# Two attention stages in a written order, with value matmuls side by side, and maximum matmuls over 65 partitions

## The chip, the cores and the metric

The kernel runs on one core of one Trainium2 chip. The metric is device time in microseconds (us), the median of timed executions; lower is better. Beside the timed executions there is one profiled execution, and every row below comes from it. The engines are TensorE (PE in the profile; PEld is its weight load), VectorE (DVE), ScalarE (ACT), GpSimd (POOL) and SyncE (SP, which issues most transfers).

## The reference

Three layers follow one another on inputs of 2 batches with 768 tokens each.

```python
# 1: attention, 8 heads of 64, a query sees the keys of its own hash bucket
q_bits = (np.einsum('bhsd,dk->bhsk', q, proj) > 0)
k_bits = (np.einsum('bhsd,dk->bhsk', k, proj) > 0)
mask = q_bucket[:, :, :, None] == k_bucket[:, :, None, :]
scores = np.where(mask, scale * np.matmul(q, k.transpose(0, 1, 3, 2)), -1e9)
attn = np.exp(scores - np.max(scores, axis=-1, keepdims=True))
attn = attn / (np.sum(attn, axis=-1, keepdims=True) + 1e-09)
x = np.matmul(attn, v)
# 2: one of 8 experts per token, 512 -> 1024 -> 512
out[b, s] = p[e] * (np.maximum(x[b, s] @ w1[e], 0.0) @ w2[e])
# 3: causal attention, 4 heads that a gate mixes (2 of 4 per token)
scores = np.where(causal, -1e9, scale * (q @ k.transpose(0, 2, 1)))
a = np.exp(scores - scores.max(-1, keepdims=True))
a /= a.sum(-1, keepdims=True) + 1e-09
out += mask[..., None] * w[:, :, kk:kk + 1] * (a @ v @ wo[e])
```

## The kernel before

There are three stages, one after another: the first attention (`stage_a`), the experts (`StageB`) and the causal attention (`StageC`, "the last stage").

The first attention is cut into 8 units `u`, each one batch and a pair of heads. A unit has two halves `qh` of 384 queries. Half by half it does: `bits` (the hash bits of a unit, tile bp, four matmuls into 32 partitions each), `mx` (12 matmuls of queries by keys, tile mp, each reduced by VectorE to a row maximum, line 338), `mneg` (VectorE joins the maxima), `mrow` (a transpose, tile mtp, whose result a transfer puts as a row into the operand of the scores), `score` (6 key tiles by 2 heads: two matmuls into tile sc, lines 360 and 362, then the exponential on ScalarE into one of six buffers pt), `av` (the value matmuls, line 372: for each of the 6 key tiles two matmuls of 64 output partitions, one a head, whose trace rows read "128*64" and "x4"), `padd` (GpSimd adds the exponentials, line 385), `sums` (two matmuls of 64 output partitions, line 394) and the steps `norm`, `rows1` (tq), `rows2` (tp) and `rows3`, which give tokens in rows for the experts.

In the last stage the four units are a batch and a pair of heads. `qk` projects, `mx` (lines 1266 and 1268) makes the row maxima: a matmul that reads 64 partitions of `U` and `K`, and on the tiles that hold the diagonal a second one over 128 partitions that adds the causal mask. `mneg` and `mrow` follow as above. `score` (lines 1302 and 1303) adds a matmul over 65 partitions, whose last row carries the maximum, and one over 128. `av` (line 1319) and `sums` (line 1337) write 64 output partitions each. `ones_row` sets row 64 of `K` to one.

All engines take their instructions in the order in which the code emits them. In both attention stages a `Plan` sets that order: each step is an item with the costs of its operations on each engine, what it depends on and the PSUM tag that it takes. `Plan.order` runs through time with these costs and always takes a ready item, by its rank (a due time, or its longest path) plus a correction from a table (`BIAS_A`, `BIAS_C`). There are three PSUM buffers each for maxima and small products, three for scores and two for value sums.

Of the kernel before, what the change touches and what calls it, by code (L numbers as in the profile page):

```python
# [35 lines left out]
LAT = 200  # L36
BIAS_C = {('av', (0, 0)): -247500, ('av', (0, 1)): -171200, ('av', (0, 1), 1): -658400, ('av', (1, 0)): -13300, ('av',
          (1, 0), 0): -14200, ('av', (1, 0), 1): -36700, ('av', (1, 1)): -13100, ('av', (1, 1), 1): -63200, ('avc',
          (1, 0)): -141100, ('causal', (1, 0)): 18900, ('gate3', 0): -59400, ('gmul', (0, 0), 0): -2700, ('mneg', (1,
          0), 1): -13800, ('mneg', (1, 1)): 43100, ('mrow', (0, 0), 0): -45100, ('mrow', (0, 0), 1): 150800, ('mx',  # L40
          (0, 0)): 1900, ('mx', (0, 0), 0): -1800, ('mx', (0, 0), 1): -1500, ('mx', (0, 1)): -138300, ('mx', (0, 1),
          1): -4300, ('mx', (1, 0), 1): 11500, ('mx', (1, 1), 1): 96800, ('norm', (0, 0), 1): -1711800, ('norm', (0,
          1), 0): 36400, ('norm', (1, 0)): 143200, ('outp', 0): -950900, ('padd', (1, 0), 0): 40600, ('padd', (1, 1),
          1): 93000, ('qk', (0, 0)): 198800, ('qk', (0, 1)): 151700, ('qk', (1, 0), 0): 25700, ('qk', (1, 0), 1):
          36900, ('qk', (1, 1)): -779000, ('qk', (1, 1), 0): -78900, ('recip', (0, 0), 1): -73000, ('recip', (0, 1),
          0): 55100, ('recip', (0, 1), 1): 28800, ('recip', (1, 1)): 168400, ('scale', 0): 41600, ('scale', 0, 5):
          418900, ('scale', 1, 0): 198900, ('score', (0, 0), 0): -124500, ('score', (0, 1), 0): -36500, ('score', (0,
          1), 1): 14400, ('score', (1, 0)): -914000, ('score', (1, 0), 1): -700, ('score', (1, 1)): -2700, ('score',
          (1, 1), 0): -10900, ('sums', (0, 0)): -17500, ('sums', (0, 0), 0): -20000, ('sums', (0, 0), 1): 44200,
          ('sums', (0, 1)): -941300, ('sums', (1, 0), 0): -79400, ('trans', 0): 625600, ('trans', 0, 0): -873600,  # L50
          ('trans', 1, 0): -425200, ('trans', 1, 3): 2100, ('vproj', 0): 3800, ('vproj', 0, 1): 300, ('vproj', 0, 2):
          450700, ('vproj', 0, 3): -800, ('vproj', 0, 4): 113400, ('vproj', 0, 5): -152300, ('vproj', 1): -544300,
          ('vproj', 1, 3): 518900}
BIAS_A = {('av', 0): -441400, ('av', 1): -227900, ('av', 1, 10): 145300, ('av', 2): -155300, ('av', 2, 11): -253100,
          ('av', 2, 5): 287900, ('av', 2, 7): -66000, ('av', 3): -69900, ('av', 3, 0): 340800, ('av', 4): -439500,
          ('av', 5): -251300, ('av', 5, 5): -25300, ('av', 5, 9): -42600, ('av', 6): -406300, ('av', 6, 4): -18400,
          ('av', 7): -549000, ('bits', 1): 304700, ('bits', 2): 134400, ('bits', 3): 6200, ('bits', 4): -3000,
          ('bits', 5): -700, ('bits0', 0): -47900, ('bits0', 1): 317700, ('bits0', 1, 1): -14700, ('consts',): -50500,
          ('fill', 1): 3700, ('hot', 0): -394600, ('hot', 1): 155000, ('kbits', 1): -54300, ('kbits', 2): -127900,
          ('kbits', 2, 0): -54500, ('kbits', 3): 13200, ('kbits', 3, 0): 14700, ('kbits', 3, 1): 154400, ('kbits', 4):  # L60
          -179100, ('kbits', 4, 0): -27100, ('kbits', 4, 1): -267600, ('kbits', 6, 1): -326300, ('kbits', 7): -352800,
          ('load', 0, 3): 429100, ('load', 2): -59000, ('load', 2, 3): 22500, ('load', 4, 1): -7500, ('load', 5, 3):
          -164600, ('loadp', 4, 1): 42300, ('loadp', 6): -23000, ('loadp', 7): 33000, ('mneg', 0): 132200, ('mneg', 1,
          0): 35300, ('mneg', 2): 45100, ('mneg', 3, 0): -247200, ('mneg', 4): -79200, ('mneg', 7, 0): -33300,
          ('mrow', 0): 253400, ('mrow', 1, 1): 7100, ('mrow', 4): 109500, ('mrow', 5): -26600, ('mrow', 6, 1):
# [3 lines left out]
          70300, ('mx', 7): -159600, ('mx', 7, 0): 4500, ('norm', 0): 9300, ('padd', 7): 39000, ('pick', 0): -12500,  # L69
          ('place', 0): -97900, ('proj', 0): 182000, ('proj', 1): 177500, ('qbits', 2, 0): -60800, ('qbits', 3):  # L70
# [4 lines left out]
          2): -68800, ('score', 0, 10): -214000, ('score', 0, 11): -216800, ('score', 0, 2): -75700, ('score', 0, 4):  # L75
          -88100, ('score', 0, 5): -53200, ('score', 0, 8): -132900, ('score', 0, 9): 26600, ('score', 1): -88500,
          ('score', 1, 0): 406700, ('score', 1, 10): -270100, ('score', 1, 6): 7300, ('score', 1, 8): -14200,
          ('score', 2): -14200, ('score', 2, 0): -84800, ('score', 2, 6): -63800, ('score', 2, 8): -123900, ('score',
          2, 9): -173400, ('score', 3): -301000, ('score', 3, 0): -52900, ('score', 3, 10): 77000, ('score', 3, 6):
          524400, ('score', 3, 7): -66300, ('score', 4): -116800, ('score', 4, 1): -19900, ('score', 4, 3): -105200,  # L80
          ('score', 5): -154900, ('score', 5, 10): -41600, ('score', 5, 5): -20700, ('score', 6): -35000, ('score', 7,
          5): 10400, ('split', 2): -283600, ('split', 2, 2): 18100, ('split', 2, 3): 17500, ('split', 3): -200700,
          ('split', 3, 3): 203900, ('split', 4): -13900, ('split', 4, 1): -2500, ('split', 5): -552500, ('split2', 1):
          -176100, ('split2', 1, 1): 434000, ('split2', 2): -40200, ('split2', 2, 3): -360300, ('split2', 3): 26800,
          ('split2', 3, 1): -690800, ('split2', 3, 3): 11500, ('split2', 4): -95000, ('split2', 6): -289600,
          ('split2', 7): -844800, ('sumc', 1, 0): 132700, ('sumc', 2, 0): -141800, ('sumc', 6): -20600, ('sums', 0):
          20500, ('sums', 0, 1): -11900, ('sums', 6, 0): -120000, ('tally', 1): -839400, ('xtrans', 1): -124100,
          ('zrow', 5): -161500}


class Plan:
    """Puts items with dependencies in an order in which each engine, taking its work in that order, waits little.
    An item has a function, its operations [(engine, ns)] (no engine: time alone), the keys that it waits for, the
    time from its last operation until others can use what it made, the PSUM bank (a tag) that it takes, for its
    own time or until the item `hold` is over, and when it is due (else: its longest path to the end counts)."""

    def __init__(self, banks):
        self.items, self.banks = {}, banks

    def add(self, key, fn, ops, deps=(), tail=0, bank=None, hold=None, due=None):  # L100
        self.items[key] = dict(fn=fn, ops=ops, deps=list(dict.fromkeys(deps)), tail=tail, bank=bank, hold=hold, due=due)

    def order(self, bias={}):
        its = self.items
        users = {k: [] for k in its}
        for k, i in its.items():
            for d in i["deps"]:
                users[d].append(k)
        rank = {}
        for k0 in its:  # L110
            todo = [k0]
            while todo:
# [19 lines left out]
        while ready:  # L132
            can = []
            for k in ready:
                i = its[k]
                t = when[k]
                if i["bank"]:
                    t = max(t, min(bank[i["bank"]]))
# [53 lines left out]
def stage_a(tc, ctx, g, q, k, v, pb):  # L192
# [10 lines left out]
    NB = 3  # L203
# [1406 lines left out]
```

## Time and profile before

| what | us |
|---|---|
| median of 3 timed runs | 658.07 (653.83 to 662.89) |
| span of the profiled execution, first to last instruction | 673.8 |
| first attention, from the span's start to about | 286 |
| experts, 286 to about 477 | 191 |
| last stage, 477 to the end | 197 |

The profile gives no time for the profiled execution beyond its span. It is 15.7 us longer than the median of the timed runs and 10.9 us longer than the slowest of them. The stages end where the last instruction that belongs to them starts. In a row of the timeline the first number is the start and the second the duration; matmuls are pipelined, so the cost of one is read from its start to the next one's start, not from its duration. A row with "x4" merges four records of one line: two value matmuls of fp32 data leave two records each.

### The profile page before, as it was taken

To read this page: it belongs to the slowest core of one execution; us is meant where nothing else is said; L and a number is where in the kernel's file an instruction comes from. 1 tells how busy PE (TensorE), PEld (TensorE's weight loads), DVE (VectorE), ACT (ScalarE), POOL (GpSimd) and SP (SyncE) were. 2 spreads that over 40 slices of the span, in tenths; PEclk is the share of its full clock that TensorE was granted. 3 is DMA by queue.
4 is the path that set the end of the run, shared out by engine and by line. 5 is a ranking of instruction groups with operands and counts; after the bars stand their busy time and mean duration, and the time that the engine had idled before them with its cause. 6 is when DMAs were issued, how large, how long until landed. Compare 5 with 4: busy or idle time off the path is not lost. (4 is left out here: it accounts for less than half of the span.)

```text
span 673.8 us, 9869 instructions
## 1 busy us (share of the span) xinstructions
PE 647.6 (96%) x3525; PEld 455.3 (68%) x3525; DVE 457.7 (68%) x889; ACT 362.8 (54%) x661; POOL 254.3 (38%) x261
## 2 busy tenths in 40 slices
PE   8989999988999899999999999999999999999997
PEld 3545656555565455799899889979797586674555
DVE  6989788887889786666666767555457445465474
ACT  6887878858586444255555455444444134142443
POOL 8584586554865654510000000000620421534561
PEclk7999999999999999999999999999999587796589
DMA  8552625624326303156665575555360001210023
GB/s 238 201 194 66 227 84 177 211 78 154 95 70 199 133 17 110 48 202 220 250 223 206 201 277 196 211 190 201 114 180 9 0 18 31 49 47 1 23 73 141
DMA packets 55639, 90.39 MB, mean 134 GB/s; under 512 B 4244, under 2 KB 28944, under 8 KB 55328
## 3 DMA queue, kind: packets, MB, share of 16 engines
q1 hardware_dynamic: 53632, 83.36, 37.2%
q0 software_dynamic: 1952, 6.34, 2.9%
q8 instruction: 29, 0.48, 0.3%
q14 instruction: 26, 0.21, 0.1%
HBM read 66.18 MB, written 20.26 MB: 128 GB/s over the span
## 5 line engine op out<-in xcount | busy, mean ns | idle before, releaser
L385 POOL TENSOR_TENSOR acc<-acc,pt 128x768 f32<-128x768 f32 x56 | 109.7, 1966 | 41.4 <-ACT pt L363 39.2
L363 ACT ACTIVATE pt<-sc 128x384 f32<-128x384 f32 x192 | 84.6, 488 | 52.4 <-PE sc L362 47.7
L338 DVE TENSOR_REDUCE m<-mp 128x1 f32<-128x384 f32 x192 | 97.4, 549 | 17.5 <-PE mp L337 16.7
L923 DVE TENSOR_TENSOR wlo<-wraw,whi 128x1024 fp32r<-128x1024 f32 x64 | 76.7, 1239 | 13.8 <-ACT whi L922 13.8
L1143 POOL DMA_INDIRECT xg<-ys,slot x12 | 11.8, 979 | 190.3 <-DVE wl L1123 184.6
L372 PE MATMUL av<-pt,vt 128*64 128x385 f32 (+1 forms) x384 | 80.4, 508 | 0.6 <-DVE xt L415 0.6
L337 PE MATMUL mp<-km,qm 128*128 128x384 f32 x192 | 67.2, 397 | 4.6 <-DVE m L338 3.0
L360 PE MATMUL sc<-qm,km 128*128 128x384 f32 x192 | 69.5, 362 | 0.5 <-ACT pt L363 0.5
L922 ACT ACTIVATE whi<-wraw 128x1024 fp32r<-128x1024 f32 x64 | 64.3, 1055 | 10.4 <-DMA wraw<-in_w_dram 5.4
L362 PE MATMUL sc<-q,k 128*128 128x384 f32 x192 | 64.6, 337 | 0.0
L963 PE MATMUL hp<-xth,whi 128*128 128x256 f32 x224 | 63.1, 282 | 1.4 <-DVEq L1091 1.4
L964 PE MATMUL hp<-xtl,whi 128*128 128x256 f32 x224 | 63.1, 281 | 0.0
L965 PE MATMUL hp<-xth,wlo 128*128 128x256 f32 x224 | 62.9, 281 | 0.0
L337 PEld LDWEIGHTS mp<-km,qm 128*128 128x128 f32 x192 | 35.1, 194 | 40.0 <-DVE m L338 23.6
L981 PE MATMUL yp<-whi,hh 128*128 128x512 f32 x128 | 51.5, 402 | 0.0
L1269 DVE TENSOR_REDUCE cm<-cmp 128x1 f32<-128x320 f32 (+3 forms) x64 | 30.9, 505 | 28.8 <-PE cmp L1268 20.9
L982 PE MATMUL yp<-wlo,hh 128*128 128x512 f32 x128 | 50.4, 393 | 0.0
L983 PE MATMUL yp<-whi,hl 128*128 128x512 f32 x128 | 50.3, 393 | 0.0
L1304 ACT ACTIVATE cp<-csc 128x384 f32<-128x384 f32 (+2 forms) x72 | 28.3, 423 | 38.6 <-PE csc L1303 35.0
L1308 POOL TENSOR_SCALAR_AFFINE_SELECT cp<-cp 128x128 f32<-128x128 f32 x48 | 13.8, 297 | 89.5 <-ACT cp L1304 89.4
L360 PEld LDWEIGHTS sc<-qm,km 128*128 128x128 f32 x192 | 36.1, 188 | 16.8 <-issue 10.2
L963 PEld LDWEIGHTS hp<-xth,whi 128*128 128x128 f32 x224 | 42.2, 188 | 2.1 <-issue 1.8
(264 smaller groups left out, 1439.0 us busy)
## 6 DMA issues: line engine op xcount, KB each, us to landing
wraw<-in_w_dram SPq DMA_DIRECT2D x32, 1024.0 KB
xs<-zt SPq DMA_DIRECT2D x13, 512.0 KB
x<-in_q_dram SPq DMA_DIRECT2D x14, 384.0 KB
x<-in_k_dram SPq DMA_DIRECT2D x14, 384.0 KB
xsb<-xs SPq DMA_DIRECT2D x7, 512.0 KB
ys<-ysb SPq DMA_DIRECT2D x7, 512.0 KB
vt<-in_v_dram SPq DMA_DIRECT2D x8, 384.0 KB
out_dram<-cos SPq DMA_DIRECT2D x12, 256.0 KB
```

What stands on the lines that cost most here:

```text
L337: nc.tensor.matmul(mp, QM[i][:, o:o + 128], KM[i][:, h * S + c * HS:h * S + (c + 1) * HS], start=True, stop=True)
L338: nc.vector.tensor_reduce(s["m"][:, qh, h, t, c:c + 1], mp, axis=AX.X, op=ALU.max)
L360: nc.tensor.matmul(sc, KM[i][:, h * S + kt * 128:h * S + kt * 128 + 128], QM[i][:, (2 * qh + h) * HS:(2 * qh + h + 1) * HS], start=True, s ...
L362: nc.tensor.matmul(sc, K1[i][:, h, ks], Q1[i][:, h, qs], start=False, stop=True)
L363: nc.scalar.activation(PT[(u * 12 + x) % NPB][:, h, :HS], sc, AF.Exp, scale=SCALE)
L372: nc.tensor.matmul(s["av", qh][64 * h:64 * h + 64, :HS + 1 - qh], s["v"][:, h, kt, :], P[:, h, :HS + 1 - qh], start=kt == 0, stop=kt == NK ...
L385: (nc.vector if u == NU - 1 else nc.gpsimd).tensor_add(s["acc", qh], p, P)
L922: nc.scalar.activation(hi[:, s], r[:, s], AF.Copy)
L923: nc.vector.tensor_sub(lo[:, s], r[:, s], hi[:, s].bitcast(F32))
L963: nc.tensor.matmul(p[:, f2, :], hi, xh[:, k, :], start=k == 0, stop=False)
L964: nc.tensor.matmul(p[:, f2, :], hi, xl[:, k, :], start=False, stop=False)
L965: nc.tensor.matmul(p[:, f2, :], lo, xh[:, k, :], start=False, stop=k == 3)
```

## The change

The change replaces the planner. `Plan.run` takes a list of item numbers (`ORDER_A` with 1007 items, `ORDER_C` with 434) and emits the items in this order, after a check that each comes behind what it depends on. The costs in the items are edited too, but nothing reads them any more. The same items exist before and after; but for the edits below only their order differs. The experts' stage keeps its order.

In the last stage, `mx` reads partitions 0 to 64 of `U` and `K` (65 instead of 64). Row 64 of `K` is now zero, the row of ones moves to 65, the row of maxima moves to row 65 of `Q`, and the score matmul reads 66 partitions instead of 65. So `ones_row` clears two rows of two tiles on GpSimd and fetches the ones by a transfer, once for each of four buffers; the `Q` tiles become four fixed buffers. `conv_w` can be emitted in halves with other items between them.

```diff
-    def run(self, bias={}):
-        for k in self.order(bias):
-            self.items[k]["fn"]()
+    def run(self, order):
+        keys = list(self.items)
+        assert sorted(order) == list(range(len(keys)))
+        seen = set()
+        for n in order:
+            i = self.items[keys[n]]
+            assert seen.issuperset(i["deps"])
+            seen.add(keys[n])
+            i["fn"]()
...
-    pl.run(BIAS_A)
+    pl.run(ORDER_A)
...
-        self.kmt = [self.p.tile([128, S], F32R, name=f"ckm{i}") for i in range(4)]
+        self.kmt, self.qmt = ([self.p.tile([128, S], F32R, name=f"{n}{i}") for i in range(4)] for n in ("ckm", "cqm"))
...
-        self.nc.gpsimd.memset(self.kmt[i][64:65].bitcast(F32), 1.0)
+
+        for t in (self.kmt, self.qmt):
+            self.nc.gpsimd.memset(t[i][64:66].bitcast(F32), 0.0)
+        self.nc.sync.dma_start(self.kmt[i][65:66].rearrange("o (a n) -> o a n", n=64).bitcast(F32),
+                               self.g["ones"][0:1, None, :].to_broadcast([1, 12, 64]))
...
-        nc.tensor.matmul(p[:, :w], s["U"][0:64, 128 * i:128 * i + 128], s["K"][0:64, k0:k1], start=True, stop=not diag)
+        nc.tensor.matmul(p[:, :w], s["U"][0:65, 128 * i:128 * i + 128], s["K"][0:65, k0:k1], start=True, stop=not diag)
...
-            nc.sync.dma_start(self.u[u, x]["Q"][64:65, HS * h:HS * h + HS].rearrange("o (t n) -> o t n", n=128).bitcast(F32),
+            nc.sync.dma_start(self.u[u, x]["Q"][65:66, HS * h:HS * h + HS].rearrange("o (t n) -> o t n", n=128).bitcast(F32),
...
-        nc.tensor.matmul(p[:, :w], s["K"][0:65, ks], s["Q"][0:65, q0:q1], start=True, stop=False)
+        nc.tensor.matmul(p[:, :w], s["K"][0:66, ks], s["Q"][0:66, q0:q1], start=True, stop=False)
...
-            sc.plan().run(BIAS_C)
+            sc.plan().run(ORDER_C)
```

The order on TensorE in the first attention, at the value matmuls of the first half of the third unit (inputs of 385 columns; av is the value sum, mp a maximum tile, mtp the transposed maxima, sm the sums, sc a score). Before:

```order
L372 MATMUL av<-pt_115,vt 64x385 x2
L337 MATMUL mp<-km_112,qm_111 128x384
L307 MATMUL bp<-xp_863,pbt 32x384 x2
L307 MATMUL bp<-xp_834,pbt 32x384 x2
L421 MATMUL tq<-ident,ss 128x128 x3
L337 MATMUL mp<-km_104,qm_103 128x384
L372 MATMUL av<-pt_116,vt 64x385 x2
L349 MATMUL mtp<-ident,mn 6x128
L372 MATMUL av<-pt_120,vt 64x384 x2
L434 MATMUL tp<-wglt,xt 128x146 x3
L394 MATMUL sm<-acc,ones 64x384 x2
L360 MATMUL sc<-qm_111,km_112 128x384
```

After:

```order
L271 MATMUL mp<-km_104,qm_103 128x384
L368 MATMUL tp<-wglt,xt 128x146 x3
L283 MATMUL mtp<-ident,mn 6x128
L306 MATMUL av<-pt_115,vt 64x385 x2
L306 MATMUL av<-pt_119,vt 64x384 x2
L306 MATMUL av<-pt_116,vt 64x385 x2
L328 MATMUL sm<-acc,ones 64x384 x2
L306 MATMUL av<-pt_117,vt 64x385 x2
L306 MATMUL av<-pt_120,vt 64x384 x2
L306 MATMUL av<-pt_118,vt 64x385 x2
L271 MATMUL mp<-km_104,qm_103 128x384 x3
L294 MATMUL sc<-qm_111,km_112 128x384
```

The value matmuls that stood apart, with maxima, transposes and scores between them, now stand in one row with the sums, right behind the transpose of the maxima.

The order on TensorE in the last stage, in the first unit (cmp is a maximum tile, with the mask matmul of identb behind it, cav the value sum, cmt the transposed maxima, ctp transposed tokens). Before:

```order
L1319 MATMUL cav<-cp_6948,cv 64x384
L1319 MATMUL cav<-cp_6886,cv 64x384
L1266 MATMUL cmp<-ckm_6465,cu_6697 128x320
L1268 LDWEIGHTS identb
L1268 MATMUL cmp<-mb,identb 128x128
L1266 MATMUL cmp<-ckm_6465,cu_6697 128x384
L1319 MATMUL cav<-cp_6954,cv 64x384
L1319 MATMUL cav<-cp_6891,cv 64x384
L1266 MATMUL cmp<-ckm_6465,cu_6697 128x256
L1268 LDWEIGHTS identb
```

After:

```order
L1253 MATMUL cav<-cp_6998,cv 64x384
L1253 MATMUL cav<-cp_7031,cv 64x384
L1221 MATMUL cmt<-ident,cmn 6x128
L1097 MATMUL ctp<-ident,xg 128x128 x8
L1253 MATMUL cav<-cp_6907,cv 64x384
L1253 MATMUL cav<-cp_7007,cv 64x384
L1253 MATMUL cav<-cp_6920,cv 64x256
L1253 MATMUL cav<-cp_6956,cv 64x256
L1253 MATMUL cav<-cp_7026,cv 64x256
L1253 MATMUL cav<-cp_6937,cv 64x256
L1253 MATMUL cav<-cp_6998,cv 64x128
L1253 MATMUL cav<-cp_7031,cv 64x128
```

The value matmuls alternated with maximum matmuls; now ten of them (the row goes on with two more) follow one another.

## Rows read from the trace of the kernel before

**Rows 1.** The page: busy time of the engines, and the granted clock by slice.

```profile
PE 647.6 (96%) x3525; PEld 455.3 (68%) x3525; DVE 457.7 (68%) x889; ACT 362.8 (54%) x661; POOL 254.3 (38%) x261
...
PEclk7999999999999999999999999999999587796589
```

**Rows 2.** By stage: window, its length, busy us of each engine (instructions), granted clock.

```profile
24.00:272.00 248.00, 232.18 (x1247) 137.73 (x1249) 206.43 (x438) 173.44 (x331) 149.51 (x90) 1.00 0.40 132
...
477.00:674.00 197.00, 191.45 (x904) 130.10 (x904) 104.92 (x209) 76.43 (x184) 71.48 (x119) 0.83 0.20 57
```

**Rows 3.** Timeline of TensorE, first attention: start us, us, line, operation, output<-inputs.

```profile
107.17 0.34 PE L362 MATMUL sc<-q,k 128*128 128x384 f32 x1
107.44 0.87 PE L372 MATMUL av<-pt,vt 128*64 128x384 f32 x4
108.23 0.45 PE L337 MATMUL mp<-km,qm 128*128 128x384 f32 x1
108.52 0.33 PE L360 MATMUL sc<-qm,km 128*128 128x384 f32 x1
108.69 0.33 PE L362 MATMUL sc<-q,k 128*128 128x384 f32 x1
```

**Rows 4.** Timeline of TensorE: value and sum matmuls that follow one another.

```profile
266.08 0.87 PE L394 MATMUL sm<-acc,ones 128*64 128x384 f32 x4
266.77 0.81 PE L372 MATMUL av<-pt,vt 128*64 128x384 f32 x4
267.42 0.81 PE L394 MATMUL sm<-pt,ones 128*64 128x384 f32 x4
```

**Rows 5.** The last stage by windows that end where the granted clock changes.

```profile
504.00:524.10 20.10, 20.10 (x118) 14.94 (x119) 14.39 (x32) 9.94 (x27) 1.70 (x6) 1.00 0.05 11
524.10:544.60 20.50, 20.50 (x66) 11.15 (x66) 7.50 (x21) 2.48 (x8) 11.77 (x20) 0.50 0.00 0
...
565.10:582.10 17.00, 17.00 (x51) 8.47 (x50) 8.53 (x19) 3.61 (x9) 3.28 (x8) 0.50 0.01 2
...
612.90:643.60 30.70, 30.70 (x99) 17.23 (x99) 13.41 (x24) 12.47 (x32) 14.92 (x31) 0.50 0.12 27
```

**Rows 6.** Timeline of TensorE, last stage, full clock: maximum matmuls.

```profile
512.90 0.43 PE L1266 MATMUL cmp<-ckm,cu 64*128 64x384 f32 x1
513.26 0.23 PE L1268 MATMUL cmp<-mb,identb 128*128 128x128 bf16 x1
513.42 0.32 PE L1266 MATMUL cmp<-ckm,cu 64*128 64x128 f32 x1
```

**Rows 7.** Timeline of TensorE, last stage, full clock: scores around a maximum matmul.

```profile
558.64 0.34 PE L1302 MATMUL csc<-cq,ckm 65*128 65x384 f32 x1
558.82 0.34 PE L1303 MATMUL csc<-cu,cv 128*128 128x384 f32 x1
...
559.87 0.23 PE L1268 MATMUL cmp<-mb,identb 128*128 128x128 bf16 x1
559.91 0.42 PE L1302 MATMUL csc<-cq,ckm 65*128 65x384 f32 x1
```

**Rows 8.** Timeline of TensorE, last stage, at half clock.

```profile
531.28 0.69 PE L1266 MATMUL cmp<-ckm,cu 64*128 64x384 f32 x1
531.89 0.29 PE L1268 MATMUL cmp<-mb,identb 128*128 128x128 bf16 x1
532.11 0.69 PE L1266 MATMUL cmp<-ckm,cu 64*128 64x384 f32 x1
```

**Rows 9.** Groups in 24 to 272 us: operation, tile, count, busy us, mean ns, idle before.

```profile
L385 POOL TENSOR_TENSOR acc<-acc,pt 128x768 f32<-128x768 f32 x56 | 109.7, 1966 | 41.4 <-ACT pt L363 39.2
L338 DVE TENSOR_REDUCE m<-mp 128x1 f32<-128x384 f32 x174 | 88.8, 549 | 17.2 <-PE mp L337 16.5
```

**Rows 10.** Groups in 477 to 674 us.

```profile
L1269 DVE TENSOR_REDUCE cm<-cmp 128x1 f32<-128x320 f32 (+3 forms) x64 | 30.9, 505 | 28.8 <-PE cmp L1268 20.9 <-PE cmp L1266 7.1
...
L1135 POOL MEMSET ckm<- 1x768 f32 x4 | 3.0, 803 | 0.0
```

More of the change, by code (lines that the diff above doesn't have):

```diff
@@ L33 @@
 WN = 2064
[L36 to L53, printed above, removed]
@@ L91 @@
+ORDER_A = [
[44 rows of a table added]
+ORDER_C = [
[19 rows of a table added]
 class Plan:
@@ L574, in stage_a @@
                     for w in X:
[L575 removed]
+                        add(bits0, h, c, w, at=-2 + h if c > w else -10 + 2.4 * h + .4 * (c + w), ops=[("PE", 640, "S"), ("DVE", 660)], bank="mx",
                             deps=[("load", 0, 2 * h + w), ("proj", 0), ("proj", 1)] + [("mneg", 0, 0)] * (c > w))
         if u:
[L578 removed]
+            add(bits, u, at=o - 20 + 6 * (u == 1), ops=[("PE", 640, "Q"), ("DVE", 470)], bank="mx",
                 deps=[("loadp", u, w) for w in X] + [("mneg", 0, 0)] + ([(f, u - 1, *x) for f, x in MOVES] if u > 1 else []))
             for c in X:
[L581 removed]
+                add(qbits, u, c, at=o - 17 + c + 6 * (u == 1), ops=[("ACT", 934)], deps=[("bits", u), ("fixed", u % NB)] + seen)
                 for h in X:
[L583 removed]
+                    add(kbits, u, c, h, at=o - 17 + c + h / 2 + 6 * (u == 1), ops=[("ACT", 608)],
                         deps=[("bits", u), ("fixed", u % NB)] + seen)
@@ L597, in stage_a @@
             e = o - 6 + 6 * qh if u else 3.1 * qh - 3.2
-            add(mneg, u, qh, at=e, ops=[("DVE", 350)], deps=[("mx", u, qh, n) for n in range(12)] + last("mrow"))
+            add(mneg, u, qh, at=e, ops=[("DVE", 270, "p")], deps=[("mx", u, qh, n) for n in range(12)] + last("mrow"))
             add(mrow, u, qh, at=e + .1, ops=[("PE", 110 if u + qh else 213), ("DVE", 200)] + dma(10), deps=[("mneg", u, qh), idn], bank="mx",
@@ L913, in conv_w @@
         nc = self.nc
-        if part == 1:
-            r, hi, lo = self.half
-        else:
-            r = self.raw.pop((e, n, c))
-            hi, lo = self.conv_tiles(e, n, c)
-        self.half = r, hi, lo
+        if (e, n, c) not in self.wt:
+            self.wt[e, n, c] = self.conv_tiles(e, n, c)
+        r, (hi, lo) = self.raw[e, n, c], self.wt[e, n, c]
         for i in range(2) if part is None else (part,):
@@ L1388, in add @@
             pl.add((name, *a), lambda: getattr(self, name)(*a), ops, deps, **kw)
-        mm = lambda w: max(w, 256) / 2.4 + 3
-        DIAG = 107
-        MM4 = lambda w: w / 0.6 + 56
+        mm = lambda w: max(w / 2.22 + 2, 110)
+        DIAG = 62
+        MM4 = lambda w: w * 635 / 384
         for i in range(4):
-            add("ones_row", i, ops=[("Pool", 675)])
+            add("ones_row", i, ops=[("Pool", 1400), ("SP", 500)], tail=2000)
         for b in range(B):
@@ L1461, in plan @@
                     dep = [("vproj", 1, i) for i in T] + [("qk", y, x, c) for y in us[2:] for x in X for c in X]
-                add("norm", u, h, ops=[("DVE", 500), ("ACT", 413), ("DVE", 500)], deps=[("recip", u, h, c) for c in range(3)] + [("gmul", u, h)] + dep)
+                add("norm", u, h, ops=[("DVE", 535, "p"), ("ACT", 415), ("DVE", 485, "p")], deps=[("recip", u, h, c) for c in range(3)] + [("gmul", u, h)] + dep)
         return pl
```

189 lines of the change are left out of this document (37 added, 152 removed), and 70 rows, old and new, of tables (BIAS_A, ORDER_A, ORDER_C).

## The prediction, made before the result

> **What bounds the kernel now.** I read the page first: TensorE is busy for 647.6 of 673.8 us, VectorE for 457.7 [rows 1]. The reader should see two more things in it: no engine but TensorE is near its limit over the span, and the line of granted clocks falls below full speed near the end. So the question is not who waits for TensorE but what it spends its time on. "Busy" doesn't mean "streaming": in the timeline the steps from start to start show it.
>
> In the first attention a score or maximum matmul steps by 0.17 us (108.52 to 108.69) [rows 3]. A pair of value matmuls that stands alone costs more than its own work. From the score ahead of it to its start are 0.27 us (107.17 to 107.44) where 0.17 is usual, the pair takes 0.79 (107.44 to 108.23), and the maximum matmul behind it takes 0.29 (108.23 to 108.52) instead of 0.17 [rows 3]. Where such pairs follow one another, one takes 0.65 us (266.77 to 267.42) [rows 4]. So a stretch of them costs 0.10 + 0.14 + 0.12 = 0.36 us for going into the 64-column form and out of it, however many pairs it holds.
>
> In the last stage the same is seen with 64 rows. A maximum matmul of 384 columns and its mask matmul take 0.36 + 0.16 = 0.52 us [rows 6]. A 65-row score matmul of 384 columns takes 0.18, and from a mask matmul to a 65-row matmul are 0.04 [rows 7]. Put together, the pair would take 0.22 if it were priced like its neighbours, so 0.30 us of 0.52 go to the change of form. It is the change between 64 and 128 rows that costs: 65 rows followed by 128 rows show no such step [rows 7].
>
> Third, the clock. In the last stage the lower level, 1.2 GHz, is granted from 524.1 to 544.6, 565.1 to 582.1 and 612.9 to 643.6 us, 68.2 us together [rows 5]. In the 20.10 us before the first fall TensorE was busy all the time, without a gap [rows 5], and what it did were mostly maximum matmuls with their changes of form. In the first attention from 24 us on the clock was full [rows 2].
>
> The Trainium skill (TensorE: Matmul & The Clock Gate, Part 1) has the clock fall after an idle window. This trace shows a fall with no idle time of TensorE ahead of it, so here the measurement decides.
>
> **The change part by part.** (1) *First attention, value matmuls together.* In the program order of before, value and sum matmuls stand in 91 separate stretches, after it in 26. 65 stretches fewer by 0.36 us are 23 us of TensorE time, and TensorE sets the end here: 232 of 248 us busy [rows 2]. Not all of it arrives. VectorE is busy for 206 of the 248 us, 83% [rows 2]; at 225 us it would be 92%, and its 174 reductions of 0.549 us for the maxima [rows 9] wait now for matmuls (16.5 us), later the matmuls will wait for them. While a row of six value pairs and a sum pair runs (7 x 0.65 = 4.6 us), no maxima and no scores are made, so VectorE and ScalarE have to have other work in that time. They have: splits, bits, normalization. I take two thirds, 16 us, with ends at 8 (VectorE full at 240) and 23. GpSimd is no bound: its additions wait 39.2 us for exponentials [rows 9]. The six buffers pt hold the exponentials until row and addition are through; a half's five additions take 5 x 1.97 = 9.8 us [rows 9], less than the 15.5 us that a half takes (248 / 16), so the scores behind a row find free buffers. The row covers a transfer, too: the transpose of the maxima stands ahead of it and the first score that needs them behind it.
>
> (2) *Last stage, 65 rows.* The 64-row matmuls stand in 58 stretches in the order of before and in none after. 48 of the 64 have a mask matmul: 48 x 0.30 = 14.4 us, and 16 without one at 0.10 each (the step into it) are 1.6 us: 16 us at full clock. Reading 65 or 66 rows instead of 64 or 65 adds nothing, by the 0.18 us of the 65-row score [rows 7].
>
> The Trainium skill (TensorEngine Tiling (Array Packing), Theoretical Speedup) speaks against this edit: with a contraction of at most 64 two tiles can work side by side, up to 2x. By that the edit would give up half of 64 x 0.2 us, about 6 us, as an estimate. Here all of these matmuls read the same partitions 0 to 63, and the rows show them one after the other [rows 6], so nothing is given up.
>
> (3) *Last stage, value matmuls together.* 33 stretches become 10: 23 x 0.36 = 8 us.
>
> (4) *The clock.* At half clock the same pair of maximum and mask takes 0.61 + 0.22 = 0.83 us, 1.6 times the 0.52 at full clock [rows 6, 8]. Streams without change of form would go 2 times as long. With 1.7, the 68.2 us of half clock hold 40 us of work at full clock: 28 us. They come back if the falls go. I expect that most do, since what stood ahead of the falls, the alternation of 64-row and 128-row matmuls, is gone; the bounds are 0 and 28.
>
> (5) *New waits in the last stage.* VectorE needs 0.505 us for a maximum [rows 10], TensorE after the change about 0.22. Ten maximum matmuls that now stand in a row take at least 5 us instead of 2.2. Over all 64, VectorE needs 30.9 us, spread over a stage in which it is busy 105 of 197 us [rows 2, 10]. Exponentials, transfers and additions will come late at places, too, as TensorE has hidden them so far. No row prices this; I take 10 us, between 0 and 20.
>
> (6) *ones_row.* Eight clearings of 0.8 us on GpSimd instead of four [rows 10], and four small transfers at the head of SP's queue of the stage. On GpSimd the second batch's gathers are queued behind them, and only its transposes wait for those; on TensorE the first batch's transposes and projections stand ahead of the first maxima. So: zero. Without that cover it is 3.2 us. *conv_w, fixed Q buffers*: the order of the experts doesn't change, zero.
>
> The sum, against the profiled execution: first attention -16; last stage -16 - 8 - 28 + 10 = -42. 673.8 - 58 = **616 us**. The median of the timed runs lies 15.7 us below the span. They vary by 9 us among themselves, which a fixed program would hardly do at a fixed clock; so I take it that they had fewer stretches at half clock than the profiled one. Then the part that I take from (4) is partly missing in them already, but the result without such stretches is the same 616. If recording is what makes the profiled execution longer, the timed result is 600.
>
> **The rivals.**
> A, *VectorE becomes the bound of the first attention.* It must reduce maxima and has 83% of the time taken already. Then (1) brings 8 us instead of 16, or less, and the waits in the last stage are 15 instead of 10: 629 us. For it: 83% is an average with its waits for TensorE inside. Against it: some of VectorE's work lies where the rows of value matmuls will be.
> B, *the clock falls as before.* It is only argued that the alternation of forms brings the falls on; it may be the maxima themselves, whose operands fill half the partitions as before, and with VectorE late at ten maxima in a row TensorE waits as well. Then (4) brings nothing and of (2) and (3) the work at half clock stays slow: 673.8 - 16 - 24 + 10 = 644, less some 7 us if the timed runs have only part of those stretches: 637. The skill's rule of an idle window (same page and part) would give this too, if the new waits are long.
> C, *the change of form is not what costs.* If weights that come late, not the form, cost the 0.30, 65 rows leave it. Then (2) brings nothing and the falls stay: 673.8 - 16 - 8 = 650, less the part of the falls that the timed runs lack, about 8: 642. Against it: 65 to 128 rows has no such step [rows 7].
> D, *slower.* Rows of value matmuls and the mixed rows of scores and maxima take turns, and VectorE and ScalarE stop during each value row, because the six buffers are full and what they have else comes at the wrong time. It costs up to the row's 4.6 us for each of 16 halves, 74 us; from 58 / 16 = 3.6 us a half on it takes all that the change gains. With the full 4.6 it is 616 + 74 = 690 us. Against it: in the order of after the items of other units stand around the rows, and the transfer is covered.
>
> **How the numbers follow.** Forecast 0.52, A 0.17, B 0.17, C 0.08, D 0.06. A measurement of this kernel tells about 2% from no change, so 645 and 671 us are the borders. The forecast and A lie wholly below 645; B and C do by more than half (0.15 of their 0.25), the rest is "same", and D gives 0.03 same and 0.03 slower. Faster 0.84, same 0.13, slower 0.03. The range goes from 600 (recording, or all of the 23 us and no new waits) to 640, which takes in A and most of B.
>
> **What would show it.** In the profile after: steps from a maximum matmul to its mask matmul of 0.18 us or VectorE's pace where they stand in a row; rows of value pairs at 0.65 us a pair; first attention until about 270 us; the last stage 150 to 160 us long and no more than one stretch at 1.2 GHz in it; VectorE busy around 90% in the first attention. I am wrong if TensorE shows idle time of more than 20 us in the first attention, named after VectorE's maxima or ScalarE's exponentials, or if the clock falls as often as before.

## The result, and the profile after

The changed kernel takes 635.5 us (median of 4 runs, 633.74 to 641.02) against 658.58 us of the kernel before on the same chip (653.83 to 662.89): ratio 0.965, 95% interval 0.958 to 0.973. It is faster by more than a measurement can miss, inside the range given, and 19.5 us above the forecast of 616.

The profiled execution has a span of 634.4 us (its own time is 636.07, so recording costs nothing). Against the 673.8 us of before it is 39.4 us shorter, more than the medians differ. The reason is the clock: the same program of before takes 659.92 us in one run at a mean granted clock of 0.968 and 674.69 in another at 0.938, and the profiled execution of before, at 0.942, is near the latter.

| stage (profiled execution) | before, us | after, us | at half clock before | at half clock after |
|---|---|---|---|---|
| first attention, with the loading at the start | 285.9 | 284.1 | 10.2 | 27.3 |
| experts | 191.6 | 191.3 | 0 | 0 |
| last stage | 196.2 | 158.9 | 68.3 | 4.8 |

(Here and below, a stage begins where TensorE's first instruction of it starts, and time at half clock is counted up to the last instruction.)

So the last stage gave nearly all of it, and the first attention, from which 16 us were expected, 1.8. The page of the kernel after, busy time of the engines and granted clock (they answer to [rows 1]):

```profile
PE 588.3 (93%) x3525; PEld 457.5 (72%) x3525; DVE 470.9 (74%) x889; ACT 366.8 (58%) x661; POOL 257.8 (41%) x265
...
PEclk8689899899989999999999999999999999999999
```

TensorE is busy for 59 us less, but the span shrank by 39 only: it waits more than before. The clock is near full in the last stage, and now has small dents in the first third. By stage (the columns are those of [rows 2]):

```profile
24.00:262.00 238.00, 211.74 (x1203) 148.82 (x1203) 216.29 (x435) 174.62 (x320) 148.46 (x96) 0.97 0.41 133
475.40:634.30 158.90, 146.70 (x904) 117.29 (x904) 104.92 (x209) 76.19 (x184) 75.35 (x122) 0.99 0.25 70
```

In the first attention VectorE is now the busiest engine: 216.3 of 238 us, 91%, where before it had 206.4 of 248 [rows 2]. TensorE idles for 26 us. Whom it waits for there, the five largest (engine, tile and line that wait, what released them: us, times, longest; xr comes from `rows3`, mn from `mneg`, bt from `bits`, r from `rows1`, m is a maximum):

```profile
PE mp L271 <- DVE xr L388: 8.0, 5, 2.3
PE mtp L283 <- DVE mn L279: 4.3, 4, 2.5
PE mp L271 <- DVE bt L243: 2.0, 3, 1.3
PE rp L684 <- DVE r L359: 1.9, 1, 1.9
PE mp L271 <- DVE m L272: 1.8, 1, 1.8
```

All five are VectorE, and the maxima m, which the prediction named, are the least of them. The rows of value matmuls are there, and they do what was expected of them (timeline of TensorE, first attention; they answer to [rows 3, 4]):

```profile
127.05 0.33 PE L296 MATMUL sc<-q,k 128*128 128x384 f32 x1
127.31 0.87 PE L306 MATMUL av<-pt,vt 128*64 128x385 f32 x4
128.00 0.81 PE L328 MATMUL sm<-acc,ones 128*64 128x384 f32 x4
128.65 3.40 PE L306 MATMUL av<-pt,vt 128*64 128x385 f32 x20
131.98 0.62 PE L271 MATMUL mp<-km,qm 128*128 128x384 f32 x2
```

Five pairs take 3.33 us from 128.65 to 131.98, 0.67 each, and the price of going in is paid once for seven pairs. The saving on TensorE is real; it turned into idle time.

In the last stage the alternation of forms is gone (timeline of TensorE, full clock; answers to [rows 6, 7]):

```profile
517.83 0.28 PE L1200 MATMUL cmp<-ckm,cu 65*128 65x256 f32 x1
517.95 0.23 PE L1202 MATMUL cmp<-mb,identb 128*128 128x128 bf16 x1
517.99 0.42 PE L1200 MATMUL cmp<-ckm,cu 65*128 65x384 f32 x1
518.25 0.23 PE L1202 MATMUL cmp<-mb,identb 128*128 128x128 bf16 x1
518.29 0.42 PE L1236 MATMUL csc<-cqm,ckm 66*128 66x384 f32 x1
518.56 0.34 PE L1237 MATMUL csc<-cu,cv 128*128 128x384 f32 x1
...
524.20 0.34 PE L1200 MATMUL cmp<-ckm,cu 65*128 65x384 f32 x1
524.38 0.23 PE L1202 MATMUL cmp<-mb,identb 128*128 128x128 bf16 x1
```

A maximum of 384 columns and its mask take 0.26 + 0.04 = 0.30 us (517.99 to 518.29), where they took 0.52 with 64 rows [rows 6], and not the 0.22 that the prediction put. The 0.04 behind a bf16 mask matmul is only a part of its price: the fp32 matmul behind it steps by 0.26 or 0.27 instead of the 0.18 that it has elsewhere (524.20 to 524.38).

### The profile page after: what moved, and what is told of

The parts are those of the page before. It is cut to its first block, busy times and chain, and to the rows that moved or that the text cites. A ratio compares the mean times of both kernels' runs of the same rounds, so it can differ in the third digit from the quotient of the medians.

```text
span 634.4 us, 9829 instructions
## 1 busy us (share of the span) xinstructions
PE 588.3 (93%) x3525; PEld 457.5 (72%) x3525; DVE 470.9 (74%) x889; ACT 366.8 (58%) x661; POOL 257.8 (41%) x265
## 5 line engine op out<-in xcount | busy, mean ns | idle before, releaser
L319 POOL TENSOR_TENSOR acc<-acc,pt 128x768 f32<-128x768 f32 x56 | 108.0, 1930 | 70.1 <-ACT pt L297 68.2
L297 ACT ACTIVATE pt<-sc 128x384 f32<-128x384 f32 x192 | 86.7, 487 | 41.3 <-PE sc L296 38.9
L854 DVE TENSOR_TENSOR wlo<-wraw,whi 128x1024 fp32r<-128x1024 f32 x64 | 76.9, 1240 | 14.2 <-ACT whi L853 14.1
L271 PE MATMUL mp<-km,qm 128*128 128x384 f32 x192 | 68.6, 393 | 15.2 <-DVE xr L388 8.0
L306 PE MATMUL av<-pt,vt 128*64 128x384 f32 (+1 forms) x384 | 70.9, 493 | 0.0
L296 PE MATMUL sc<-q,k 128*128 128x384 f32 x192 | 67.5, 351 | 0.0
L271 PEld LDWEIGHTS mp<-km,qm 128*128 128x128 f32 x192 | 38.0, 203 | 34.9 <-issue 10.9
L306 PEld LDWEIGHTS av<-pt,vt 128*64 128x64 f32 x384 | 25.6, 136 | 30.1 <-issue 26.1
L898 ACT ACTIVATE hh<-hp 128x512 fp32r<-128x512 f32 x32 | 19.2, 599 | 43.4 <-PE hp L895 43.2
L1262 POOL TENSOR_TENSOR cp<-cp,cp 128x384 f32<-128x384 f32 (+2 forms) x49 | 39.4, 825 | 7.5 <-PE cav L1253 6.6
L894 PEld LDWEIGHTS hp<-xtl,whi 128*128 128x128 f32 x224 | 42.2, 188 | 0.2
```

The lines of the kernel that those rows point to most:

```text
L271: nc.tensor.matmul(mp, QM[i][:, o:o + 128], KM[i][:, h * S + c * HS:h * S + (c + 1) * HS], start=True, stop=True)
L296: nc.tensor.matmul(sc, K1[i][:, h, ks], Q1[i][:, h, qs], start=False, stop=True)
L297: nc.scalar.activation(PT[(u * 12 + x) % NPB][:, h, :HS], sc, AF.Exp, scale=SCALE)
L306: nc.tensor.matmul(s["av", qh][64 * h:64 * h + 64, :HS + 1 - qh], s["v"][:, h, kt, :], P[:, h, :HS + 1 - qh], start=kt == 0, stop=kt == NK ...
L319: (nc.vector if u == NU - 1 else nc.gpsimd).tensor_add(s["acc", qh], p, P)
L854: nc.vector.tensor_sub(lo[:, s], r[:, s], hi[:, s].bitcast(F32))
```

## The experiments

### Which part of the change brings the last stage's gain

**c_65_only**: the kernel before in its own orders, with the 65 rows alone.

```diff
-        nc.tensor.matmul(p[:, :w], s["U"][0:64, 128 * i:128 * i + 128], s["K"][0:64, k0:k1], start=True, stop=not diag)
+        nc.tensor.matmul(p[:, :w], s["U"][0:65, 128 * i:128 * i + 128], s["K"][0:65, k0:k1], start=True, stop=not diag)
...
-                Q=self.p.tile([128, S], F32R, name=f"cq{x}", bufs=2), K=self.kmt[(2 * (2 * b + pp) + x) % 4])
+                Q=self.qmt[(2 * (2 * b + pp) + x) % 4], K=self.kmt[(2 * (2 * b + pp) + x) % 4])
```

> The kernel before with the 65-row edit of the last stage alone, both orders as before. If the change between 64 and 128 rows is what costs, the last stage loses 16 us of change of form and most of its half clock: 625 to 640 us, the maximum matmul to its mask matmul at 0.18 us. If it is late weights (rival C of the prediction), no more than 5 us off 658. If the clock falls without the change of form as well (rival B), about 642 us with stretches at 1.2 GHz of 30 us or more.

Measured: 637.17 us (636.31 to 639.17), ratio 0.966 (0.959 to 0.972); last stage 156.2 us with 1.7 at half clock, first attention 287.7. This one edit brings as much as the whole change, and the last stage lost its stretches at half clock with it.

**c_order_only**: 64 rows, the old order in the first attention, the written order in the last stage.

```diff
-            sc.plan().run(BIAS_C)
+            sc.plan().run_list(ORDER_C)
```

> The kernel before with the written order of the last stage alone, 64 rows, first attention in the old order. By the changes of form, only the 23 stretches of value matmuls go: 8 us, 650 us, and the clock falls as before since 64-row and 128-row matmuls still alternate. If the order is worth more by itself (shorter chains), 640 us or less.

Measured: 676.2 us (674.96 to 683.11), ratio 1.028 (1.017 to 1.038), not the 650 expected. This doesn't show a loss of that size: its four executions had mean granted clocks of 0.934 to 0.951, and with 0.937 to 0.943 the kernel before takes 674.9 to 679.8 us. Last stage 195.1 us, with 63.2 at half clock. The stretches of value matmuls are together in it as in the kernel after, and the clock falls as before.

**c_both_a_old**: both edits of the last stage, the first attention in the old order.

> Both edits of the last stage, first attention in the old order. If the new order of the first attention is worth nothing, as the end of that stage in the profile after says (284 us against 286), this is as fast as the changed kernel: 632 to 640 us. If the new order does save TensorE time there and something else takes it, for instance the clock, it is 5 to 10 us slower than the changed kernel.

Measured: 639.81 us (638.94 to 640.9), ratio 0.970 (0.964 to 0.976); last stage 159.7 us, 3.5 more than with the 65 rows alone, with 9.3 at half clock; first attention 285.6.

**a_new_c_old**: the reverse: the new order of the first attention, the last stage as before.

```diff
-            sc.plan().run(ORDER_C)
+            sc.plan().run_bias(BIAS_C)
```

> The written order of the first attention alone, last stage as before. If that order is worth nothing by itself, 655 to 660 us, with the first attention ending at 284 us. If its worth was hidden by what the last stage does, 645 us or less.

Measured: 660.93 us (650.02 to 674.09, 10 runs), ratio 0.992 (0.984 to 1.000); first attention 282.5 us. In the profiled execution the last stage took 175.6 us with 21.7 at half clock.

This last stage is the same program as that of before, and so are those of b_half_split and b_one_add, below; only the clock differs. That gives the price of half clock from rows:

| last stage with 64 rows, old order | us | at half clock |
|---|---|---|
| before | 196.2 | 68.3 |
| b_one_add | 191.0 | 54.6 |
| a_new_c_old | 175.6 | 21.7 |
| b_half_split | 173.1 | 14.9 |

From the first to the third line 20.6 us go with 46.6 us of half clock, 0.442 each; the other two lie within 0.9 us of that line. At the 1.7 us of half clock that c_65_only has, the stage with 64 rows would take 175.6 - 0.442 x 20.0 = 166.8 us. So of the 40 us between before and c_65_only, 29.4 are clock and 10.6 change of form.

What the written order adds is seen by windows of the last stage. First c_65_only, and whom TensorE waits for in it:

```profile
479.70:635.80 156.10, 150.19 (x904) 114.03 (x904) 104.32 (x208) 74.84 (x184) 74.33 (x122) 0.99 0.25 71
...
PE cqp L1248 <- DVE cxl L1171: 0.9, 1, 0.9
```

Then the same waits in the kernel after, whose window stands above:

```profile
PE cqp L1179 <- DVE cxl L1102: 3.8, 1, 3.8
PE ctp L1097 <- DVE xg L1090: 1.4, 2, 1.3
PE cav L1253 <- POOL cp L1242: 1.3, 1, 1.3
```

TensorE is busy for 146.7 us instead of 150.2, so the order does save 3.5 us of it; but it idles for 12.2 instead of 5.9. The largest new wait, 2.9 us longer, is that of the projection for VectorE's split at the head of the stage, and a stretch at half clock follows it (last section). The loss is no scatter: with 65 rows the written order took 157.9 to 159.7 us in six kernels, the old one 156.2 to 156.6 in three. The six had 3.5 to 9.3 us at half clock, the three 0 to 1.7; at 0.442 us each that would be most of the difference, an estimate.

### What holds the first attention

**a_half_split** and **b_half_split**: in the kernel after and in the one before, VectorE's subtraction that splits queries and keys covers half the columns; the other half is left out.

```diff
-        e.tensor_sub(X1[lo], x[lo], X1[lo].bitcast(F32))
+        e.tensor_sub(X1[lo, :HS], x[lo, :HS], X1[lo, :HS].bitcast(F32))
```

> The changed kernel with half of each subtraction of the operand splits of the first attention left out (28 VectorE operations over 384 of 768 columns, so the scores are other numbers). This takes some 20 us of VectorE's work. If VectorE has become the bound of the first attention, that stage ends 10 us or more earlier than at 284 us. If TensorE at a dipping clock or the chain of steps bounds it, 0 to 4 us earlier.

> The same cut in the kernel before. If TensorE and its changes of form bound the first attention there, it ends 0 to 5 us earlier than at 286 us; if VectorE bounds it there too, 10 us or more.

Measured: first attention 273.2 us instead of 284.1 in the kernel after, 279.5 instead of 285.9 in the one before. Less work for VectorE makes both faster, the kernel after more; the 6.4 us of the kernel before lie between its two expectations. The subtraction on k went from 1690 ns to 1354 only, that on q from 1268 to 908, though they have half the columns: a good part of their time isn't their own work.

**a_one_add**: the kernel after, with 56 of the 70 additions on GpSimd left out.

```diff
-        (nc.vector if u == NU - 1 else nc.gpsimd).tensor_add(s["acc", qh], p, P)
+        if kt == 1 or u == NU - 1:
+            (nc.vector if u == NU - 1 else nc.gpsimd).tensor_add(s["acc", qh], p, P)
```

> The changed kernel with GpSimd's additions of exponentials left out but for the first of each half (56 of 70 go, sums are too small). If VectorE bounds the first attention and its operations are stretched by GpSimd's, VectorE's mean times for the split subtractions fall from 1.6 us to about 1.0 and the stage ends 10 us or more earlier than at 284 us. If nothing of it bounds, 0 to 3 us.

Measured: first attention 253.8 us, 30.3 less; the whole 605.58 us. No instruction of VectorE was touched. Its groups in the kernel after (the last columns: busy us, mean ns of one, idle before):

```profile
L272 DVE TENSOR_REDUCE m<-mp 128x1 f32<-128x384 f32 x179 | 89.8, 548 | 8.6 <-PE mp L271 7.9
L235 DVE TENSOR_TENSOR k<-x,k 64x768 fp32r<-64x768 f32 x13 | 21.8, 1690 | 0.4
L278 DVE TENSOR_TENSOR mn<-m 128x6 f32<-128x6 f32 x15 | 10.4, 693 | 0.3
L279 DVE TENSOR_SCALAR mn<-mn 128x6 f32<-128x6 f32 x15 | 10.3, 685 | 0.5
```

The same groups with 56 additions fewer:

```profile
L272 DVE TENSOR_REDUCE m<-mp 128x1 f32<-128x384 f32 x179 | 89.9, 549 | 9.0 <-PE mp L271 8.2
L235 DVE TENSOR_TENSOR k<-x,k 64x768 fp32r<-64x768 f32 x14 | 13.3, 955 | 4.3 <-ACT k L233 3.9
L278 DVE TENSOR_TENSOR mn<-m 128x6 f32<-128x6 f32 x15 | 4.0, 268 | 0.3
L279 DVE TENSOR_SCALAR mn<-mn 128x6 f32<-128x6 f32 x15 | 4.2, 277 | 0.5
```

The subtraction on k and the small operations on `mn`, which read SBUF, shrink to 0.57 and 0.4 of their time (that on q from 1268 to 985 ns); the maxima, which read PSUM, take 549 ns either way. Over the whole first attention the same 520 instructions keep VectorE busy for 247.3 us in the kernel after and for 208.1 without the additions. The timeline of the kernel after shows how. An operation on `mn` that starts during an addition on GpSimd lasts until that addition ends, one that meets none takes 0.16 or 0.17 us:

```profile
122.64 1.84 POOL L319 TENSOR_TENSOR acc<-acc,pt 128x768 f32<-128x768 f32 x1 [2.06 <-ACT pt L297]
122.66 1.84 DVE L278 TENSOR_TENSOR mn<-m 128x6 f32<-128x6 f32 x1
124.53 0.17 DVE L279 TENSOR_SCALAR mn<-mn 128x6 f32<-128x6 f32 x1
```

All 15 of the 32 operations on `mn` that took over 0.2 us started during a GpSimd instruction and ended 0.02 or 0.03 us after it. So VectorE's 91% were in part waiting for GpSimd, inside its instructions. Another reading, that the results of the additions come earlier or their buffers come free earlier, isn't borne out by the waits: between 24 and 250 us TensorE names an addition once, for 2.3 us at a weight load, and ScalarE never. The Trainium skill (SBUF — State Buffer, SBUF: two separate sides) says that VectorE and GpSimd share a pair of ports, and that whichever of certain operations starts first holds it for its whole instruction. The trace agrees, by the rows above: 1.84 us beside an addition and 0.16 or 0.17 without one, for an operation of six columns.

**a_few_av**: the kernel after, with 64 of the 96 pairs of value matmuls left out (tokens go to other experts by it, so only the first attention tells).

```diff
-        for h in range(2):
+        for h in range(2) if kt in (0, NKT - 1) else ():
             nc.tensor.matmul(s["av", qh][64 * h:64 * h + 64, :HS + 1 - qh], s["v"][:, h, kt, :], P[:, h, :HS + 1 - qh],
```

> The changed kernel with value matmuls for two of six key tiles only (64 of 96 pairs left out): 64 x 0.65 = 42 us of TensorE work less. If VectorE bounds the first attention, it ends less than 10 us earlier than at 284 us, and TensorE idles. If TensorE still bounds it, 30 us earlier or more. If the clock dips more often for want of work, later than that.

Measured: first attention 292.1 us, not earlier than the 284.1 of the kernel after, though 64 x 0.65 = 42 us of TensorE's work are gone. TensorE idles for 52.6 of the 238 us up to 262 instead of 26.3, although the clock is at half for 51 us. TensorE doesn't set the end of this stage any more.

**b_one_add**: the cut of a_one_add in the kernel before.

> The kernel before, with 56 of its 70 GpSimd additions of exponentials left out (all but the first of each half, but for the last unit), so that the sums are of two key tiles instead of six. The same cut in the kernel after brought the first attention from 284.1 to 253.8 us. Theory (VectorE, stretched by GpSimd, sets the pace of the first attention, and this hides what the order saves on TensorE): with GpSimd out of the way TensorE is the bound again, and then the 91 separate stretches of value matmuls of the old order cost what the prediction priced them at: the first attention of this kernel ends at 265 to 277 us, 12 to 23 later than with the new order. Rival (the change of form never cost this much): it ends at 250 to 258 us, as with the new order.

Measured: first attention 267.9 us, 14.1 later than with the new order. TensorE is busy for 224.9 of 226 us (24 to 250 us; first of this kernel, then of a_one_add):

```profile
24.00:250.00 226.00, 224.87 (x1223) 136.03 (x1223) 177.20 (x437) 171.66 (x326) 38.81 (x35) 1.00 0.45 145
```

```profile
24.00:250.00 226.00, 218.87 (x1323) 153.22 (x1322) 192.73 (x484) 179.60 (x337) 50.80 (x56) 1.00 0.46 148
```

So with GpSimd out of VectorE's way the order of the first attention is worth 14 us, near the 16 of the prediction; with it in the way, some 2 to 5: four kernels with the old order and all their work took 285.6 to 287.7 us, three with the new one 282.5 to 284.1. The cut is worth 18.0 us to the old order (285.9 to 267.9) and 30.3 to the new one.

### Versions that the runs point to

**a_new_c65**: the kernel after, with the 65 rows but the planner's old order in the last stage.

> The kernel after with the last stage in the planner's old order, but with the 65 rows: the whole change without the written order of the last stage. Theory (the written order of the last stage costs about 3 us once no 64-row matmul is left): last stage 156 us, the whole 631 to 634 us, 2 to 4 us under the kernel after. Rival (the 3 us are scatter between kernels): last stage 158 to 160, the whole 635 to 637.

Measured: 632.32 us (629.99 to 635.12), ratio 0.958 (0.953 to 0.963); last stage 156.5 us, first attention 282.8. The last stage in the old order is shorter again, by 2.4 us, as the theory had it. Against c_65_only the first attention is 4.9 us shorter.

**v_direct5**: the kernel after, with the fifth of the five additions of each half replaced by two sum matmuls that read that tile directly.

```diff
+        if u == NU - 1 or kt < 5:
+            (nc.vector if u == NU - 1 else nc.gpsimd).tensor_add(s["acc", qh], p, P)
...
+        for kt in range(5, NKT) if u < NU - 1 else ():
+            P = PT[(u * 12 + 6 * qh + kt) % NPB]
+            for h in range(2):
+                nc.tensor.matmul(s["sm", qh][64 * h:64 * h + 64, :], ones, P[:, h, :HS], start=False, stop=kt == NKT - 1)
```

> The kernel after with the last of the five GpSimd additions of each half (but for the last unit) replaced by two more sum matmuls on TensorE, which read that tile of exponentials directly: 14 additions of about 2 us less on GpSimd, 14 x 0.65 = 9.1 us more on TensorE, same output. Theory (VectorE beside GpSimd sets the pace, TensorE has time to spare): the 56 additions were worth 30.3 us, 0.54 each, so 14 bring up to 7.6 us: first attention 277 to 281 us, the whole 628 to 633. Rival (TensorE is the bound of the first attention): it ends 5 to 9 us later, 289 to 293, the whole 640 to 645.

Measured: 626.13 us (623.96 to 631.81), ratio 0.949 (0.943 to 0.955), the fastest of the kernels that leave nothing out. The first attention takes 275.2 us, 8.9 less, with 9 us more work on TensorE:

```profile
24.00:250.00 226.00, 211.85 (x1238) 146.15 (x1237) 199.09 (x424) 171.62 (x314) 119.63 (x78) 0.98 0.43 139
```

TensorE's load rose from 199.7 to 211.9 us in this window, VectorE's fell from 206.3 to 199.1, and the stage got shorter. It ends earlier than the theory had it (277 to 281). Part of that may be the clock: the stage has 6.8 us at half clock against 27.3. Of the 27.3, 13.7 lie in the loading at the start; a_new_c65, whose first attention is the same program as that of the kernel after, was without them and took 282.8 us.

**v_direct4_c65**: two additions replaced, and the last stage as in a_new_c65.

> The version that the runs so far point to: the kernel after with the last two of the five GpSimd additions of each half replaced by sum matmuls that read the exponentials directly (the variant before replaced one and brought the first attention from 284.1 to 275.2 us), and with the last stage in the planner's old order with 65 rows (156.5 us in the run before, against 158.9). Theory (VectorE beside GpSimd is the bound, TensorE only its rival): with one addition replaced TensorE was busy for 212 of 226 us between 24 and 250 us; 14 more additions replaced add 14 x 0.65 = 9 us to that, so the two bounds meet and the second step brings less than the first: first attention 270 to 275 us, last stage 156 to 157, the whole 617 to 623. If every addition left out is worth the same 0.64 us whatever TensorE does: first attention 266, the whole 614. Rival (TensorE is over its limit with 18 us more): first attention 276 to 284, the whole 624 to 632.

Measured: 630.96 us (625.71 to 632.75), first attention 278.5, last stage 156.6. One of its 16 halves gets wrong sums: in `ORDER_A` an exponential of unit 6 (fifth key tile, second head) is emitted ahead of the sums of unit 5's second half, which now read the buffer that it overwrites. In all other halves the sums stand first, as they do everywhere in v_direct5. So it is no version to use as it stands, and only the times of its stages are read. The first attention is 3.3 us later than with one addition replaced, so the second step takes back some of what the first gave; TensorE is busy for 217 of 226 us in it. The figure is in the rival's range (276 to 284), but 17.1 us at half clock in this stage, against 6.8 in v_direct5, are part of it. What remains open is how much.

The last stage of a_new_c65 with the first attention of v_direct5 was not run; by its stages it would have a span of 275.2 + 190.7 + 156.5 = 622.4 us, an estimate.

## Why the prediction was right, and where not

The time fell inside the range, and the direction for the reasons given in (2) and (4). The forecast missed by 19.5 us, and the range held because it was drawn out to 640 to take in rival A (629) and most of B (637), both nearer to the result than the forecast. B's nearness is luck, since its mechanism falls (below). By the steps, from one profiled execution to the other:

| step | predicted, us | measured, us | from |
|---|---|---|---|
| (1) first attention | -16 (8 to 23) | -1.8 | 285.9 to 284.1 |
| (2) 65 rows, form | -16 | -10.6 | line through the last stages with 64 rows |
| (4) clock | -28 (0 to 28) | -29.4 | the same |
| (3) value matmuls together | -8 | -3.5 | busy time of c_65_only and after |
| (5) new waits | +10 (0 to 20) | +6.3 | idle time of the same two |
| (6) ones_row, and the experts | 0 | -0.3 | 191.6 to 191.3 |
| sum | -58 | -39.3 | |

These are 39.4 us of span; the medians differ by 23.1. The 16.3 between I put down to the lower clock of the profiled execution of before; then the medians hold some 13 of the 29.4 us of (4), an estimate. The prediction had this right: it took the time without falls, 616, for the median too.

**The step that failed is (1).** "TensorE sets the end here: 232 of 248 us busy" was only in part true of the kernel before, and not of the kernel after. In before, 18.0 of the 285.9 us go when only GpSimd's additions are cut (b_one_add). In the kernel after, 65 stretches fewer took TensorE's work away, but VectorE sets the pace from there on (and the clock falls behind its waits, 17 us more at half clock than before). That is rival A: a_few_av takes TensorE's work away and gains nothing, a_half_split takes VectorE's away and gains 11 us. The rival still expected 8 us or less, and 8 is the lower end of (1); "VectorE full at 240" doesn't follow from its 206 us, which are 86% of that. And both looked at the maxima, for whose reduction the maximum matmuls wait 1.8 us only. What neither saw is why VectorE is full: its 206 us of before were counted as work, and part of them is time in which its instructions wait for GpSimd, which the step put at nothing ("GpSimd is no bound"). With the new order more of them meet an addition: over the whole stage VectorE is busy for 247.3 us, where before it was 233.9 with the same work but for two instructions. Not every group got longer. In the kernel before these were:

```profile
L301 DVE TENSOR_TENSOR k<-x,k 64x768 fp32r<-64x768 f32 x14 | 20.4, 1455 | 2.8 <-ACT k L299 2.4
L344 DVE TENSOR_TENSOR mn<-m 128x6 f32<-128x6 f32 x15 | 11.5, 767 | 0.1
L345 DVE TENSOR_SCALAR mn<-mn 128x6 f32<-128x6 f32 x15 | 5.7, 382 | 0.5
```

1455 became 1690 and 382 became 685, but 767 became 693. The 16 us were the right size for TensorE alone: b_one_add against a_one_add gives 14.1. Of these, 12.3 were lost again to GpSimd's additions, which cost the stage 18.0 us in the old order and 30.3 in the new.

**(2) was right in its mechanism and too large.** The pair went from 0.52 to 0.30 us, not to 0.22, since a matmul behind the bf16 mask steps by 0.08 more than one behind fp32; whether the type of the mask matmul or its 128 columns make it, no run tells. 48 x 0.22 + 16 x 0.10 = 12.2 us, near the 10.6. The sign was in [rows 7] already: the score behind the mask lasts 0.42 there, the one ahead of it 0.34.

**(4) was right.** The falls go with the 64 rows: c_65_only has 1.7 us at half clock in the last stage, c_order_only 63.2. With 65 rows one fall without a wait ahead of it is left in these runs, 3.4 us at 515.2 us in c_both_a_old, where TensorE was busy for 12.0 of the 12.2 us before; in the last stage falls of 13 us and more come with 64 rows alone. Rival B falls. Whether it is the alternation of 64 and 128 rows that brings them on, as the prediction had it, or the 64 rows themselves, no run tells apart, since none has 64-row matmuls without the alternation.

**(3) and (5)** came out at +2.8 together where +2 was expected, each smaller than put. So the written order of the last stage is a small loss here, and with 64 rows it is worth nothing either (c_order_only). Rivals C and D fall: 65 rows do away with the step, and the rows of value matmuls didn't cost what D asked. Whether some of TensorE's 26 us of idle time in the first attention comes by D's way, from the rows, no run tells.

Of the signs named: the last stage of 150 to 160 us and VectorE at about 90% came; the first attention until 270 us didn't, and the idle time of over 20 us, which was to show the forecast wrong, did. It is named after VectorE, as the sign asked, but hardly after its maxima.

## What to carry to other kernels

A saving on the busiest engine is worth no more than the distance to the next one, and that one's load must be read with care: if an operation takes different times in different places (0.16 and 1.84 us for six columns), part of its "busy" time is a wait that no row names, and freeing the engine that it collides with can be worth more than the reordering (v_direct5: 8.9 us for 14 additions moved to TensorE, the clock's part in it included). Matmuls over 64 rows between others over 128 are worth a row of zeros that makes them 65: here each change cost a step, and the 64 rows the clock as well. When a change has parts, each should be timed alone: the 65 rows brought all of this one, and the list of 434 numbers beside it cost 2 to 3 us.

## What the runs showed of the hardware

The granted clock falls in two different situations here. With 64-row maxima in the last stage it falls while TensorE is busy without a gap [rows 5]. In the first attention of the kernel after it falls for 3.4 us, four times, and each time TensorE had just waited for VectorE: by 1.84, 2.33, 2.03 and 2.08 us, at 37, 64, 115 and 175 us. One of them (timeline of TensorE; in brackets the wait and what ended it):

```profile
63.59 0.44 PE L271 MATMUL mp<-km,qm 128*128 128x384 f32 x1
66.36 0.64 PE L271 MATMUL mp<-km,qm 128*128 128x384 f32 x1 [2.33 <-DVE xr L388]
66.80 0.52 PE L294 MATMUL sc<-qm,km 128*128 128x384 f32 x1
67.12 0.52 PE L296 MATMUL sc<-q,k 128*128 128x384 f32 x1
```

The scores behind it step by 0.32 us instead of 0.17. The wait of 3.76 us for `cxl` in the last stage is followed by a fifth such fall, at 489.6 us. Not every wait is followed by one: one of 2.55 us, at 91.9, isn't; and in the first attention of before, where the longest wait was 1.76 us, there is none after the loading at the start. The same program has one in c_order_only, at 61.4 us behind a wait of 1.53, and one in c_65_only, at 224.6 us behind waits of 1.19 and 0.93. By the Trainium skill (TensorE: Matmul & The Clock Gate, Part 1) the clock falls after an idle window. The trace agrees for these falls in so far as TensorE was idle ahead of each, though the length of a wait alone doesn't tell here whether a fall follows; for those of the last stage of before, with TensorE busy for 20.10 of 20.10 us [rows 5], it doesn't. So a lost wait costs TensorE twice: the wait, and the slower work behind it.
